# Linear attention feeding a mixture of experts: other queues and cast loads in the opening, one division per head pair, and a layout pass ordered by due times

## The chip, the cores and the metric

The kernel runs on one core of a Trainium2 chip. A core has five engines that run their own instruction streams and wait for each other through semaphores: TensorE (PE: matmuls, with its weight loads shown apart as PEld), VectorE (DVE), ScalarE (ACT), GpSimd (POOL) and SyncE (SP). Three of them, POOL, SP and ACT, can issue DMA transfers; 16 DMA engines carry them. TensorE writes its results to PSUM (here eight banks of 128 x 512 float32), and DVE and ACT read them from there. The metric is the time of one launch on the device in microseconds (us). Smaller is better.

## What is computed

Two stages. Linear attention with the feature map elu + 1 over 8 batches, 8 heads, 576 tokens and 64 values a head; then four experts of two layers each, weighted by a normalised table of probabilities, over the 4608 tokens of all batches:

```python
def _attn_ref(q, k, v):                 # (8, 8, 576, 64) each
    def phi(x):
        return np.where(x > 0, x, np.exp(x) - 1.0) + 1.0
    q_p, k_p = (phi(q), phi(k))
    kv = np.einsum('bhsd,bhse->bhde', k_p, v)
    z = np.sum(k_p, axis=2)
    num = np.einsum('bhsd,bhde->bhse', q_p, kv)
    den = np.einsum('bhsd,bhd->bhs', q_p, z)[..., None] + 1e-06
    return (num / den).astype(np.float32)

def _moe_ref(x, domain_probs, w1, w2):  # x (4608, 512), w1 (4, 512, 1024), w2 (4, 1024, 512)
    p = domain_probs / (domain_probs.sum(-1, keepdims=True) + 1e-09)
    out = np.zeros((N, D), dtype=np.float32)
    for e in range(E):
        h = np.maximum(x @ w1[e], 0.0)
        out += p[:, e:e + 1] * (h @ w2[e])
    return out.astype(np.float32)
```

The attention's output, with heads laid side by side, is the `x` of the second stage.

## The kernel before, in words

**Tiling.** Of the 576 tokens of a batch 512 form a main block (128 partitions of 4 tokens, index `c`) and 64 a rest. The rests of two batches share 128 partitions. Heads go in four pairs (`pr`), so that a pair fills 128 partitions of head values. Work is in float16 with float32 accumulation; the inputs are float32 in memory.

**Attention of one pair** (`attention`, line 382). Three loads bring k, v and q of the pair (`load_pair`, line 258). ACT takes exp of k and of q (412), DVE makes the feature map with two operations each (404, 405), ACT casts v to float16 beside a column of ones (408). PE multiplies k and v (`kv`, 457, and 460 for the 64 rest tokens), so that the product has 2 x 65 columns: values and the sum of k. ACT copies its two diagonal blocks (470, 471). PE transposes q (424), ACT copies the result (437), PE multiplies it by the copied blocks (481), and DVE divides: a reciprocal (495) and a product (497). In the opening the four chunks are divided in two lots, three chunks in the bank `at` and one in the bank `l2b2`. `rest_maps` (313) makes the maps of the 64 rest tokens, with an ACT cast of v (330); `rest_late` (338) finishes the rest of batch 0.

**The opening.** Batch 0 runs while weights still arrive. After each pair's division `turn_x` (579) transposes the new 128 columns of x on PE and ACT copies them (589). `first_l1` (618) then adds that pair's step of layer 1 of expert 0 for four of its eight column blocks (594: four matmuls a pair, one for each of four PSUM banks). After the fourth pair come the other four blocks, then layer 2 (`first_l2`, 655; matmuls 604, weighted sums on DVE 659 to 661). Experts 1 to 3 follow on batch 0, with the attention of batch 1 between them.

**The rest.** Batches 1 to 7 and the rests go through 64 units (`units`, 689). A unit is 256 tokens and one expert, done with seven block products instead of eight in each layer (746 and 822), with sums of weights, of x and of h on DVE. In this part the transposes of q and x are DMA transposes from SP's queue, and the pairs' loads come from SP too.

**Order.** The whole program is first written into a list by `Plan.add`, each operation with its engine, a planned duration, a priority and the keys that it reads and writes. `Plan.order` (55) lays the list out in one pass: it takes the engine that can start first, and on it, of the operations ready by then, the one with the smallest priority number. Priorities are written by hand as times: `T0` and `TU` (138) say that unit n is due at 84.0 + 6.4 n. POOL keeps the order of the list. The engines then run these orders; waits are by semaphores. POOL's DMAs use eight semaphores in turn, so a transfer is issued only when the eighth before it has landed.

**Queues in the opening** (lines 916 to 964). SP loads k, v and q of pair 0. POOL loads, in this order: the rest's k and v of batch 0, pair 1, one slice of w1 of expert 0, pair 2, a slice, pair 3, two slices, the rest's q, the probabilities (one load for the main blocks of all batches, two for the rests), w2 of expert 0, then the weights of expert 1, and so on with batch 1 between. Weights are cast to float16 by their loads. Pair 2 uses as its stage buffers the tiles `xp` and `u2`, which the units use later.

Of the kernel before, what the change touches and what calls it, by code (L numbers as in the profile page):

```python
# [17 lines left out]
BIG = 3.0e38  # L18


class Plan:
# [5 lines left out]

    HOP = 0.28
    NEAR = 0.1
# [24 lines left out]

    def order(self):
        ops = self.ops
# [18 lines left out]
        for _ in ops:  # L75
# [20 lines left out]
            if o["move"]:  # L96
                mover = max(done + o["lead"], mover) + o["move"]
                done = mover + (0.6 if mover < 80 else 2.5)
# [11 lines left out]
def kernel(  # L110
# [27 lines left out]
    T0, TU = 84.0, 6.4  # L138
# [54 lines left out]
    vss.append(u2_b[0].rearrange("p (h c d) -> p h c d", h=2, c=C))  # L193
    xt0 = s4_b[1].rearrange("p a c t -> p a (c t)")
# [63 lines left out]
    def load_pair(b, pr, queue, pri, after=0.0):  # L258
        hs = slice(2 * pr, 2 * pr + 2)
        n = 3 if b < 2 else 2  # L260
        i = rot("stage%d" % n, n) if n == 2 else rot("stage3", 3)
        stage[b, pr] = i
        kk = stage_keys(i)
        for t, o, key in ((k, kqs[i][:, 0], kk[0]), (v, vss[i], kk[2]), (q, kqs[i][:, 1], kk[1])):
            dma(queue, pri, o, t[b, hs, 0:NT].rearrange("h (p c) d -> p h c d", c=C), (key,), 0.7,
                hold=b == 2, after=after)

    def load_rest(b, queue, pri, after=0.0, parts=(0, 1, 2)):
        par = b % 2
        rs = slice(par * R, par * R + R)  # L270
        for i in parts:
            t, o = ((k, kqr[rs, 0]), (v, vr[rs]), (q, kqr[rs, 1]))[i]
            dma(queue, pri, o, t[b, :, NT:S].rearrange("h s d -> s h d"), (("str", par, i),), 0.75,
# [14 lines left out]
    def probs():  # L288
        raw = p5_b[:, 0 : B * C * E].rearrange("p (b c e) -> p b c e", b=B, c=C)
        rrest = sb("prawr", [P, B // 2, E], FP32)  # L290
        src = moe_domain_probs.rearrange("(b s) e -> s b e", s=S)
        dma("POOL", 6, raw, src[0:NT].rearrange("(p c) b e -> p b c e", c=C), ("p5",), 1.5)
        for par in range(2):
            dma("POOL", 6, rrest[par * R : (par + 1) * R],
                src[NT:S].rearrange("s (b t) e -> t s b e", t=2)[par], (("prawr", par),), 0.4)

        def go(r, o, rs, nb):
            nc.vector.tensor_reduce(out=rs, in_=r, axis=mybir.AxisListType.X, op=AO.add)
            nc.vector.tensor_scalar(rs, rs, 1e-9, None, AO.add)
            nc.vector.reciprocal(rs, rs)  # L300
            nc.vector.scalar_tensor_tensor(
                out=o, in0=r, scalar=INV, in1=rs.broadcast_to([P, nb, E]),
                op0=AO.mult, op1=AO.mult,
            )

        rs0, rs1 = sb("prs0", [P, B * C], FP32), sb("prs1", [P, B // 2], FP32)
        pl.add("DVE", 0.6, 24, lambda: go(raw.rearrange("p b c e -> p (b c) e"),
               p_nat.rearrange("p b c e -> p (b c) e"), rs0, B * C), r=("p5",), w=("pnat",))
        pl.add("DVE", 0.4, 60, lambda: go(rrest, p_rest, rs1, B // 2),
# [3 lines left out]
    def rest_maps(b, pe_mode, pri, parts=(0, 1)):  # L313
# [11 lines left out]
        for i in parts:  # L325
# [3 lines left out]
            if i == 0:  # L329
# [52 lines left out]
    def attention(b, pr, pe_mode, pri, step, two=False):  # L382
# [23 lines left out]

        def vcast():
            nc.scalar.copy(vp[:, :, :, 0:D].rearrange("p c h d -> p h c d"), vs)

        order_ = (0, 1)  # L410
        for i in order_:
# [4 lines left out]
            if i == 0:  # L416
                pl.add("ACT", 0.52, pri + step, vcast, r=(sk[2],), w=(("vp", vi),))
# [29 lines left out]
        kvs_, ndk = slot[0], (("at",), ("at",))  # L447
        nds = [slot[0:3], slot[0:2]]
        if two:
            more = [l2b[2][:, i * 2 * DE : (i + 1) * 2 * DE] for i in range(3)]  # L450
            kvs_, ndk = more[0], (("at",), ("l2b2n",))
            nds[1] = more[1:3]
        kvk = ("l2b2k",) if two else ("at",)

        def kv():
            for c in range(C):
                nc.tensor.matmul(  # L457
                    out=kvs_, lhsT=kp[:, c], rhs=vp[:, c], start=(c == 0), stop=False
                )
# [5 lines left out]
                stop=True,  # L465
            )

        def kvcopy():
# [4 lines left out]
        pl.add("PE", 0.3, pri + 4 * step, kv,  # L473
               r=(("kqp", pi, 0), ("vp", vi), ("vpr", par), "kpr"), w=kvk)
# [4 lines left out]
        def nd_mm(u, c0, n):  # L479
            for c in range(c0, c0 + n):  # L480
                nc.tensor.matmul(  # L481
                    out=nds[u][c - c0],
# [6 lines left out]
        def norm(u, c0, n, ri):  # L489
            nd = at[:, 0 : n * 2 * DE]  # L490
            if two and u:
                nd = l2b[2][:, 2 * DE : (2 + 2 * n) * DE]
            nd = nd.rearrange("p (c h e) -> p c h e", c=n, h=2)
# [9 lines left out]
            if n == 2:  # L503
# [7 lines left out]
        for u, (c0, n) in enumerate(((0, 3), (3, 1 if two else 2))):  # L511
            ri = rot("rc", 2)
            pl.add("PE", 0.06 * n, pri + (5 + u) * step, lambda u=u, c0=c0, n=n: nd_mm(u, c0, n),
                   r=(("qT", ti), ("kvz", zi)) + ((("qTr", par, pr),) if n == 2 else ()), w=ndk[u])
            pl.add("DVE", (0.5, 0.74, 0.72)[n - 1], pri + (5.5 + u) * step,
                   lambda u=u, c0=c0, n=n, ri=ri: norm(u, c0, n, ri), r=ndk[u],
                   w=[("x", par, pr, c) for c in range(c0, min(c0 + n, C))]
                   + ([("xr", b, pr)] if n == 2 else []))
# [99 lines left out]
    def first_l1(e, pri, step, wide):  # L618
        ht = []
        banks = [(l1b[i], "l1b%d" % i) for i in range(3)]  # L620
        if wide:
            banks += [(l2b[i], "l2b%d" % i) for i in range(1)]
# [7 lines left out]
        if wide:  # L630
            for dc in range(DC):
                for fj in range(4):
                    bank, key = banks[fj]
# [6 lines left out]
            done = 4  # L640
# [398 lines left out]
```

## Time and profile before

| | us |
|---|---|
| runs before: median of 3 (lowest, highest) | 502.38 (501.99, 503.30) |
| the profiled execution, its own time | 502.13 |
| its span, first to last instruction | 500.4 |

| engine | busy, us |
|---|---|
| DVE | 409.4 |
| ACT | 368.1 |
| POOL | 42.4 |

The profile's page gives busy time by engine, then the span in 40 slices of 12.5 us, where each digit is the busy share of an engine in tenths. These are the slices of the DMA engines and of the granted TensorE clock:

```profile
PEclk9999999999999999999999999999999999999999
DMA  8999957935677597465456685757622432323321
```

The DMA engines are close to full for the first five slices, in which all weights are loaded, and have room later. Below the slices the page has the chain of work that ended last and the costliest groups of instructions. A timeline row reads: start, duration, engine, line, operation, output tile <- input tiles, shape, how many; in brackets how long the engine had been idle and what ended that. Tile names come without buffer numbers: `s` can be `s15` (which also holds the identity) or `s4`, `l2b` any of four banks.

### The profile page before, as it was taken

The numbers are of one execution on the slowest core, as the hardware profiler recorded it, in microseconds if no ns is written. First come the engines' busy times: TensorE is split into PE (matmuls) and PEld (weight loads), VectorE is DVE, ScalarE is ACT, GpSimd is POOL, SyncE is SP. The second block draws the span as 40 slices with busy tenths as digits, with TensorE's granted clock in tenths as the row PEclk, the third lists the DMA queues.
The fourth block names the chain that finished last, engine by engine and source line by source line (L and its number), as shares of the span: only waits on it lengthen the run. The fifth ranks groups of instructions, "written<-read, shape, count | busy, mean of one in ns | idle before, by whom it ended". The sixth has DMA issues, their size and how long they took to land.

```text
span 500.4 us, 14836 instructions
## 1 busy us (share of the span) xinstructions
PE 480.9 (96%) x6008; PEld 423.5 (85%) x6008; DVE 409.4 (82%) x1036; ACT 368.1 (74%) x694; POOL 42.4 (8%) x68
## 2 busy tenths in 40 slices
PE   2799999999999999999999999999999999999995
PEld 1444546999999999999999999999999999999994
DVE  5787997889998999798998898899988676767664
ACT  5738667997987798859886888788866767676641
POOL 8846500000000000000000000000000000000000
PEclk9999999999999999999999999999999999999999
DMA  8999957935677597465456685757622432323321
GB/s 236 233 235 221 264 123 171 262 69 159 145 159 161 128 146 159 114 179 146 127 117 175 120 179 117 132 151 149 160 54 77 53 86 45 86 44 85 39 49 44
DMA packets 124006, 67.51 MB, mean 135 GB/s; under 512 B 94480, under 2 KB 117776, under 8 KB 123936
## 3 DMA queue, kind: packets, MB, share of 16 engines
q1 hardware_dynamic: 115056, 51.53, 46.4%
q0 software_dynamic: 8720, 14.76, 13.9%
q8 instruction: 47, 0.77, 0.6%
q10 hardware_dynamic: 160, 0.26, 0.2%
q14 instruction: 23, 0.19, 0.1%
HBM read 45.16 MB, written 9.44 MB: 109 GB/s over the span
## 4 chain that ended last, share of the span: by engine, by line
PE 90%; DMA 3%; ACT 3%; DVE 2%; issue 1%; POOL 1%; DVEq 0%; POOLq 0%; ACTq 0%
PE l1b L746 39%; PE l2b L822 37%; PE l2b L604 5%; PE l1b L594 5%; DMA w<-in_moe_w_dram 2%; PE at L481 2%; PE at L457 1%; DMA vr<-in_v_dram 1%; ACT xp L706 1%; DVE ot L661 1%; ACT h L760 0%; DVE ot L888 0%; ACT ek L412 0%; PE at L460 0%; ACT p L763 0%
## 5 line engine op out<-in xcount | busy, mean ns | idle before, releaser
L746 PEld LDWEIGHTS <-w 128*128 128x128 f16 x2048 | 132.4, 98 | 4.8
L760 ACT ACTIVATE h<-l1b 128x512 f16<-128x512 f32 x128 | 76.8, 600 | 54.0 <-PE l1b L746 52.5
L822 PE MATMUL l2b<-w,h 128*128 128x256 f16 x768 | 114.9, 273 | 0.1
L822 PE MATMUL l2b<-t,s 128*128 128x256 f16 x768 | 112.6, 273 | 0.0
L746 PEld LDWEIGHTS <-w1x 128*128 128x128 f16 x1536 | 99.9, 98 | 5.1 <-issue 1.5
L822 PEld LDWEIGHTS <-s 128*128 128x128 f16 x1024 | 92.1, 98 | 7.5
L766 DVE CUSTOM_DVE_ANT_0 h<-l1b,p 128x512 f16<-128x512 f32 x64 | 44.1, 690 | 44.9 <-PE l1b L746 40.5
L746 PE MATMUL l1b<-xs,w1x 128*128 128x128 f16 x1024 | 78.1, 219 | 0.5 <-ACT l1b L763 0.3
L746 PE MATMUL l1b<-xT,w 128*128 128x128 f16 x1024 | 78.1, 219 | 0.0
L746 PE MATMUL l1b<-xs,w 128*128 128x128 f16 x1024 | 78.1, 219 | 0.0
L706 ACT ACTIVATE xp<-x,p_nat 128x512 f16<-128x512 f16 x112 | 76.4, 720 | 1.2 <-DMA xT<-xp 0.4
L822 PEld LDWEIGHTS <-h 128*128 128x128 f16 x768 | 67.2, 98 | 5.2 <-ACT h L760 0.3
L808 DVE TENSOR_TENSOR s<-h 128x512 f16<-128x512 f16 x128 | 53.8, 420 | 1.4
L766 DVE CUSTOM_DVE_ANT_0 h<-l1b,u 128x512 f16<-128x512 f32 x64 | 43.8, 684 | 3.5 <-PE l1b L746 2.2
L763 ACT COPY u<-l1b 128x512 f32<-128x512 f32 x64 | 37.4, 584 | 12.5 <-PE l1b L746 12.2
L763 ACT COPY l1b<-l1b 128x512 f32<-128x512 f32 x64 | 36.6, 572 | 13.1 <-PE l1b L746 11.8
L763 ACT COPY p<-l1b 128x512 f32<-128x512 f32 x64 | 37.4, 584 | 8.8 <-PE l1b L746 7.6
L724 DVE TENSOR_TENSOR xs<-xT,xs 128x256 f16<-128x256 f16 x128 | 36.9, 288 | 4.1 <-DVE xs L724 0.5
L412 ACT ACTIVATE ek<-kq 128x512 f16<-128x512 f32 x60 | 37.8, 631 | 2.4 <-DMA kq<-in_k_dram 1.9
L746 PE MATMUL l1b<-xT,w1x 128*128 128x128 f16 x512 | 39.0, 219 | 0.1
L822 PE MATMUL l2b<-w,s 128*128 128x256 f16 x256 | 38.4, 273 | 0.0
L405 DVE TENSOR_TENSOR kqp<-ek,kqp 128x512 f16<-128x512 f16 x64 | 27.2, 425 | 10.6 <-ACT ek L412 7.1
(114 smaller groups left out, 560.7 us busy)
## 6 DMA issues: line engine op xcount, KB each, us to landing
w<-in_moe_w_dram POOLq DMA_DIRECT2D x32, 256.0 KB, 7.5
out_dram<-ot SPq DMA_DIRECT2D x16, 512.0 KB, 3.2
kq<-in_k_dram SPq DMA_DIRECT2D x25, 256.0 KB, 3.1
vs<-in_v_dram SPq DMA_DIRECT2D x25, 256.0 KB, 3.2
kq<-in_q_dram SPq DMA_DIRECT2D x25, 256.0 KB, 3.9
kq<-in_k_dram POOLq DMA_DIRECT2D x5, 256.0 KB, 7.2
vs<-in_v_dram POOLq DMA_DIRECT2D x5, 256.0 KB, 6.6
kq<-in_q_dram POOLq DMA_DIRECT2D x5, 256.0 KB, 6.1
```

Source lines behind the costliest of these rows:

```text
L405: nc.vector.tensor_tensor(out=o, in0=ek[:, i], in1=o, op=AO.min)
L412: pl.add("ACT", 0.55, pri + i * step, lambda i=i: nc.scalar.activation(ek[:, i], kq[:, i], AF.Exp), r=(sk[i],), w=(("ek", ei, i),))
L594: nc.tensor.matmul(out=bank, lhsT=w1_sb[e][:, dc, fj * P : (fj + 1) * P], rhs=xt0[:, dc, :], start=(dc == 0), stop=(dc == DC - 1),)
L604: nc.tensor.matmul(out=bank, lhsT=hts[ht[fj]][:, c * P : (c + 1) * P], rhs=w2_sb[e][:, fj, :], start=(fj == 0), stop=(fj == FC - 1),)
L706: pl.add("ACT", 0.6, pri, lambda c=c, src=src, ps=ps: nc.scalar.activation(xp[:, c, :], src, AF.Copy, scale=ps), r=r, w=(("xp", xi, c),))
L724: lambda o=o, a=a, b_=b_: tt(out=o, in0=a, in1=b_, op=AO.subtract),
L746: nc.tensor.matmul(out=bank[:, fc * P : (fc + 1) * P], lhsT=wt[:, kc, fc * P : (fc + 1) * P], rhs=r[:, kc, :], start=(start and fc == 0 an ...
L760: return lambda: nc.scalar.activation(o, bank, AF.Relu)
L763: return lambda: nc.scalar.copy(o, bank)
L766: return lambda: nc.vector._custom_dve(TENSOR_ADD_SAT, out=o, in0=bank, in1=t, s0=BIG, s1=0.0)
L808: pl.add("DVE", 0.36, U(n + 1) + d - 0.5, lambda i=i, a=a, b_=b_, alu=alu: tt(out=s4[:, i], in0=a, in1=b_, op=alu), r=r, w=(Q(i),))
L822: nc.tensor.matmul(out=l2b[bank][:, half * HD : (half + 1) * HD], lhsT=a[:, c, :], rhs=w[:, c], start=(opens and first and c == 0), stop=( ...
```

## The change

It has six parts.

1. **v cast by its load.** In batch 0 the v of pairs 1 to 3 is loaded from POOL's queue straight into float16 (`v16`), in the first half of its own stage buffer. The v of pair 0 still comes from SP in float32 and is cast by ACT, into `v00`. As v now has no column of ones beside it, `kv` multiplies twice per chunk: 2 x 64 columns of v and 2 columns of a constant tile `ones`.
2. **First rests on other queues.** The rest's k of batch 0 is loaded on ACT's queue, ahead of everything there. Its v is loaded by POOL, cast on the way into `vprs[0]`, behind pair 1's k. All pairs' loads now stand before the four w1 slices; then two batches of probabilities, w2, and only then the rest's q.
3. **One division per pair** in the opening: numerators of all four chunks fill `at`, denominators go to 8 columns of `l2b2`, with one reciprocal and one product for all.
4. **Probabilities in two loads**: batches 0 and 1 in the opening, batches 2 to 7 and the rests at the end of POOL's list, into a buffer that is free by then.
5. **Second layout pass by deadlines**: `order` lays the list out once, computes for each operation not on PE the latest start that still meets the PE starts of that pass, uses it as priority, and lays the list out again.
6. **Priorities and layer shapes**: `T0` becomes 79.0, hand priorities of the opening's layers and of batch 1 move, layer 2 of expert 0 takes four banks instead of three, and the memsets are regrouped.

```diff
+    LAND = 0.6
...
+    def deadlines(self):
+        ops = self.ops
+        late = [o["start"] if o["eng"] == "PE" else BIG for o in ops]
+        for n in range(len(ops) - 1, -1, -1):
+            o = ops[n]
+            for d in o["deps"]:
+                x = ops[d]
+                lat = self.HOP if x["eng"] != o["eng"] or x["move"] else 0.03
+                if x["move"]:
+                    lat += x["lead"] + x["move"] + self.LAND
+                late[d] = min(late[d], late[n] - lat - x["dur"])
+        for n, o in enumerate(ops):
+            if o["eng"] != "PE":
+                o["pri"] = late[n]
+
     def order(self):
+        self.lay_out()
+        self.deadlines()
+        return self.lay_out()
...
-    T0, TU = 84.0, 6.4
+    T0, TU = 79.0, 6.4
...
+    v00 = vss[1].rearrange("p h c d -> p (h c d)").bitcast(FP16)[:, 2 * C * D :].rearrange(
+        "p (h c d) -> p h c d", h=2, c=C
+    )
+    ones = sb("ones", [P, 2, 1], FP16)
...
+    def v16(i):
+        flat = vss[i].rearrange("p h c d -> p (h c d)").bitcast(FP16)
+        return flat[:, 0 : 2 * C * D].rearrange("p (h c d) -> p h c d", h=2, c=C)
...
-        for t, o, key in ((k, kqs[i][:, 0], kk[0]), (v, vss[i], kk[2]), (q, kqs[i][:, 1], kk[1])):
+        vo = vss[i] if b or queue == "SP" else v16(i)
+        for t, o, key in ((k, kqs[i][:, 0], kk[0]), (v, vo, kk[2]), (q, kqs[i][:, 1], kk[1])):
...
+            if first is not None and key == kk[0]:
+                first()
...
+            if b == 0 and i == 1:
+                o, key = vprs[0][rs, :, 0:D], ("vpr", 0)
...
-            if i == 0:
+            if i == 0 and b:
                 pl.add("ACT", 0.55, pri + 0.1, lambda: nc.scalar.copy(
                     vprs[par][rs, :, 0:D], vr[rs]), r=(("str", par, 1),), w=(("vpr", par),))
...
+            if two:
+                nc.scalar.copy(vh, vs)
...
-            if i == 0:
-                pl.add("ACT", 0.52, pri + step, vcast, r=(sk[2],), w=(("vp", vi),))
+            if i == 0 and not (two and pr):
+                pl.add("ACT", 0.52, pri + step, vcast, r=(sk[2],), w=(vk,))
...
+                if two:
+                    nc.tensor.matmul(out=kv3[:, :, 0:D], lhsT=kp[:, c], rhs=vh[:, :, c],
+                                     start=(c == 0), stop=False, skip_group_check=True)
+                    nc.tensor.matmul(out=kv3[:, :, D:DE], lhsT=kp[:, c], rhs=ones,
+                                     start=False, stop=False, skip_group_check=True)
...
+            def nd0():
+                for c in range(C):
+                    nc.tensor.matmul(out=at[:, c * P : (c + 1) * P], lhsT=qT[:, c],
+                                     rhs=kvz[:, :, 0:D], start=True, stop=True)
+                    nc.tensor.matmul(out=den[:, c], lhsT=qT[:, c],
+                                     rhs=kvz[:, :, D:DE], start=True, stop=True)
+
+            def norm0():
+                rc = rc4.rearrange("p (c h) -> p c h", h=2)
+                nc.vector.reciprocal(rc, den)
+                nc.vector.tensor_tensor(
+                    out=xs[:, :, fs].rearrange("p c (h d) -> p c h d", h=2),
+                    in0=at.rearrange("p (c h d) -> p c h d", c=C, h=2),
+                    in1=rc[:, :, :, None].broadcast_to([P, C, 2, D]),
+                    op=AO.mult,
+                )
...
+    load_rest(0, "ACT", 0, parts=(0,))
     load_pair(0, 0, "SP", 0)
-    load_rest(0, "POOL", 0, parts=(0, 1))
-    load_pair(0, 1, "POOL", 0)
-    load_w1(0, (0,))
+    load_pair(0, 1, "POOL", 0, first=lambda: load_rest(0, "POOL", 0, parts=(1,)))
     load_pair(0, 2, "POOL", 0)
-    load_w1(0, (1,))
     rest_maps(0, True, 3, (0,))
     for pr in range(DC):
         if pr == 3:
             load_pair(0, 3, "POOL", 0)
-            load_w1(0, (2, 3))
+            load_w1(0, range(DC))
+            probs(0, 2, p5_b, ("p5",), "pnat0", 24)
+            load_w2(0)
             load_rest(0, "POOL", 0, parts=(2,))
-            probs()
...
-    ht = first_l1(0, 7, 0.7, True)
-    first_l2(0, ht, 28, 0.9, False)
+    ht = first_l1(0, 15, 0.2, 4)
+    first_l2(0, ht, 22, 0.9, True)
...
+    xk = tuple(("xr", b, pr) for b in (6, 7) for pr in range(2))
+    probs(2, B, xr_sb[:, 3].bitcast(FP32), xk, "pnat", U(0) + 10)
+    probs_rest(U(0) + 20)
```

As laid out, PE's order in the opening changes too: the product of k and v of pair 1 now stands before the transposes of pair 0's q, and each pair's numerator matmuls alternate with 2-column ones for the denominators. PE has 32 matmuls more in all, and as many weight loads.

## The prediction

> **What bounds the kernel now.** I read the page's engine totals and slices first, then the engines' busy time by stretch, then the timeline of the opening beside the chain of waits. The page, totals and the slice row of TensorE:
>
> ```profile
> PE 480.9 (96%) x6008; PEld 423.5 (85%) x6008; DVE 409.4 (82%) x1036; ACT 368.1 (74%) x694; POOL 42.4 (8%) x68
> ...
> PE   2799999999999999999999999999999999999995
> ```
>
> TensorE is the bound nearly everywhere, and what it misses lies in the first two slices and the last. By stretch (us, then busy time and instructions of PE, PEld, DVE, ACT, POOL, then granted clock, DMA share, GB/s):
>
> ```profile
> 0.00:24.20 24.20, 11.51 (x80) 6.96 (x81) 15.87 (x52) 15.67 (x32) 20.27 (x36) 1.00 1.02 235
> 24.20:100.00 75.80, 74.66 (x545) 43.18 (x545) 64.58 (x146) 50.88 (x100) 22.10 (x33) 1.00 0.97 213
> 100.00:480.00 380.00, 379.82 (x5200) 359.69 (x5198) 318.85 (x817) 294.92 (x551) 0.00 (x0) 1.00 0.54 119
> 480.00:500.40 20.40, 14.90 (x188) 13.69 (x185) 10.12 (x24) 6.62 (x13) 0.00 (x0) 0.97 0.09 28
> ```
>
> PE idles 12.69 us up to 24.2, then 1.14 up to 100, 0.18 in the next 380 and 5.50 at the end, where the last sums and stores run. The edits don't touch the end: the last dozen instructions of PE, DVE, ACT and SP stand in the same order in both programs. So whatever is gained comes out of 12.69 + 1.14 us, and the steady part can only lose.
>
> Why 24.2: the timeline of the opening (start, us, engine, line, operation, tiles, shape, in brackets the idle time before and its releaser).
>
> ```profile
> 8.04 0.62 ACT L330 CAST vpr<-vr 64x512 f16<-64x512 f32 x1 [0.71 <-DMA vr<-in_v_dram]
> ...
> 8.71 0.27 PE L460 MATMUL l2b<-vpr,kqpr 128*128 128x130 f16 x1 [0.74 <-ACT vpr L330]
> ...
> 11.23 0.58 ACT L437 COPY qT<-l2b 128x512 f16<-128x512 f16 x1
> ...
> 17.02 0.63 PE L594 MATMUL l2b<-s,w 128*128 128x512 f16 x1
> ...
> 19.32 0.38 PE L594 MATMUL l2b<-s,w 128*128 128x512 f16 x1
> ...
> 23.61 0.58 ACT L589 COPY s<-l2b 128x512 f16<-128x512 f16 x1 [1.33 <-PE l2b L584]
> ...
> 24.25 0.81 PE L594 MATMUL l1b<-s,w 128*128 128x512 f16 x3 [0.67 <-DMA w<-in_moe_w_dram]
> ```
>
> Layer 1 of expert 0 goes in four steps, one per head pair of batch 0; from the fourth (24.25) on PE is saturated. The chain of waits puts a weight load before it:
>
> ```profile
> 12.08 6.94 DMA w<-in_moe_w_dram
> 19.02 0.29 issue
> 19.31 4.90 DMA w<-in_moe_w_dram
> 24.21 0.04 issue
> 24.25 0.81 PE l1b L594 x3
> ```
>
> I don't believe it. The slice needed here is the fourth of w1, issued at 12.08 and landed at 19.02; the transfer issued at 19.31 is of the next weights and shares a rotating semaphore. What ended at 24.19 is the ACT copy at 23.61. The opening ends with the attention of pair 3; w1 had been there for 5 us.
>
> **How the sum is made.** PE's work from that fourth step on is the same in both programs (the 32 added matmuls lie before it). So the time moves by (start of the fourth step − 24.25), plus changes of the 1.14 and 0.18 us of later idling.
>
> **Part 1: transfers.** The 16 DMA engines are full from 2.5 us on (share 1.02 over the opening), so data comes in queue order: by issue plus landing, 0.70 us per k, v or q transfer, 1.1 to 1.4 per weight slice. The rest of k moves from POOL (issued 1.29, landed 4.9 later, at 6.16) to ACT's queue at about 0.74. Before shows no ACT load; the near row is SP's load of the same rows at 78.65, which landed in 3.3: that gives 4.0; sharing with k of pair 0 at most 5. I take 4.3. ACT pays one issue of about 0.5 (SP's 0.47 here), ahead of its table load (1.28), both over before the first data: nothing, and 0.5 if data were there at 2.5. The rest of v comes already cast, behind k of pair 1: 7.96 becomes 6.3 (one 0.7 transfer less ahead would give 7.2, both less 6; the ACT cast of 0.62 goes as well). A casting load may move more or less slowly than a plain one; the near row is the w slices, 512 KB read in 1.1 to 1.4 us, the rate of the plain loads, so nothing, with −0.3 to +0.4 per pair.
>
> [...] Then six transfers of 0.70 instead of six and two w slices: q3 lands at 13.8 (before 16.51). w1 now follows all pairs: first slice 15.0 (before 11.05), fourth 18.5 (before 19.02). The first is used at 15.78 before, so 4.7 us of slack shrink to about 1.
>
> **Part 2: attention of batch 0.** Off ACT: three of four v casts (3 x 0.61) and the rest cast (0.62). DVE: a pair's two reciprocals and two products (0.19, 0.56, 0.17, 0.29; 1.19 from start to end at 20.01) become one reciprocal and one 128x512 product: 0.20 + 0.72, from 0.56 for 384 and 0.29 for 128 columns; I take 0.95 with the hop. PE: each pair gets eight 2-column matmuls, each with a weight load of its own. Row: loads of 0.10 us (0.15 cold); no 2-column matmul is shown. Bounds: hidden (0) to 0.15 each; I take 0.11 cold, 0.055 warm, so +0.4 us for kv and +0.4 for the division's matmuls, half that warm.
>
> The path, all in program order. ACT holds exp q1, kvz1's copies, exp k2 before the copy of qT0: 9.5 + 0.52 + 0.43 + 0.52 + 0.58 = 11.55 (before 11.81). Division matmuls 0.61 + 0.4: 12.6. Behind them on PE: turn q1 and kv2 (0.6 + 1.0) to 14.2, turn x0 to 14.8, division of pair 1 to 15.8, turn q2 to 16.3; x0's copy (15.4) and the first w1 slice (15.0) are there. Layer 1 step one 0.9 warm: 17.2. Then kv3 0.65, turn x1 0.25, division of pair 2 0.45 = 18.55; DVE 0.95 + hop = 19.55; turn x2 and two layer-1 matmuls 0.85, division of pair 3 0.45 = 20.85; DVE 0.95 = 21.8; turn x3 0.4, copy 0.6 = **22.8**. Before 24.25: **−1.45 us**.
>
> PE's state is the soft spot. In the rows above the same matmul takes 0.63 at 17.02 and 0.38 at 19.32 with the granted clock at 1.00 throughout. [...]
>
> **Part 3: later weights.** Earlier arrival doesn't help if layer 1 of expert 1 stands waiting. [...] Expert 3's w1 is complete at 63.1 and used at 68.15: 5 us of slack. DVE's w sums stay covered: PE first needs them at 82.
>
> **Part 4: probabilities, memsets, T0.** The opening's four DVE operations (1.09 in sum) shrink to about 0.6 and stand after pair 3's product: off the path. The second load (POOL, idle after 60) is needed from batch 2 on, past 100. Memsets stay before 4.3. All 0. T0 only shifts priorities.
>
> **Part 5: second pass.** It reorders DVE, ACT and SP everywhere. To gain: of the 1.14 us, waits of 0.59 (67.7) and 0.27 (83.9). I take −0.6 in 24 to 100 (bounds −1.1 and +1.5), 0 in the steady part (−0.18 to +6, below). Store and load order on SP is hidden behind loads that are issued tens of us early; a transpose of x behind a late store would cost PE its wait in full.
>
> **Sum.** −1.45 − 0.6 = −2.05: span 500.4 → 498.35. The profiled execution took 502.13, 1.7 more than its span, and the median is 502.38: **500.1 us**, −0.45%. About 0.3% (1.5 us) is what a measurement of this kernel can tell from no change.
>
> **Rivals.**
> A, the forecast: 0.40, 499.0 to 501.2.
> B, more: PE is fast early, pairs run through without ACT's order holding them, both idle rests vanish: fourth step at 21 to 21.5 and −1.1: 497.0 to 498.5, limit by part 3. For it: ACT had 8.5 us idle in the opening. Against: its order puts loads' exps before qT copies. 0.20.
> C, hidden anyway: q0 slips to 9, PE stays cold and runs 32 more matmuls; fourth step at 23.8 to 24.5, rest as before: 501.2 to 503.5. For it: DMA full, part 2's PE additions. 0.23.
> D, slower: the second pass ranks by due times from planned durations that are too short (DVE sums 0.36 planned, 0.42 in the row, four per unit; relu sums 0.62 and 0.69, two per unit: 0.38 us of DVE per unit). Work is then placed that much too late and the steady part gets a wait per unit. 64 units at 0.1 us: +6.4, less 2: 506.5. It decides from 0.06 per unit, 3.5 us between 100 and 480. For it: DVE 84% busy there. Against: 61 us of DVE air, and PE's order alternates the two layers more evenly in the new program. 0.17.
>
> Chances: faster = B + nearly all of A = 0.57; same = C and A's tail = 0.26; slower = D = 0.17. The range, 497.0 to 503.6, leaves out D's far side and little of B; A alone is 499.0 to 501.2.
>
> **What would show it.** Right: k rest landed by 5, q3 by 14.5; step one of layer 1 waiting for neither w1 nor DMA; fourth step at 22.3 to 23.6; idle of PE in 24:100 under 1.1 and in 100:480 under 0.5. Wrong: first step waiting for its w1 slice (then everything behind it on PE waits, kv3 and the pairs too), layer 1 of expert 1 waiting for DMA, or idle of PE beyond 3 us in 100:480.

## The result and the profile after

| us | median | lowest to highest | runs |
|---|---|---|---|
| before | 502.25 | 501.99 to 503.30 | 4 |
| after | 499.63 | 499.00 to 500.29 | 4 |

The ratio is 0.9944, with a 95% interval of 0.9925 to 0.9963: 2.6 us faster, and the forecast of 500.1 lies 0.5 us above the measured median. The profiled execution took 499.62 with a span of 497.8 (before 502.13 and 500.4). The same kernel, run once more beside the experiments, gave 499.26.

The page after, the rows of TensorE in the totals and the slices:

```profile
PE 479.3 (96%) x6040; PEld 424.8 (85%) x6040; DVE 411.1 (83%) x1033; ACT 366.9 (74%) x690; POOL 42.5 (9%) x68
...
PE   1899999999999999999999999999999999999995
```

PE has its 32 matmuls more and is still bound nearly everywhere; the slices are too coarse to show where 2.5 us went. The busy time by stretch, cut at the start of the fourth step of layer 1 (columns as before: PE, PEld, DVE, ACT, POOL, granted clock, DMA share, GB/s):

```profile
0.00:22.75 22.75, 10.70 (x112) 7.88 (x113) 14.26 (x44) 13.31 (x27) 16.76 (x30) 1.00 1.07 215
22.75:100.00 77.25, 76.55 (x578) 45.28 (x578) 66.78 (x155) 53.75 (x105) 25.70 (x38) 1.00 0.99 214
100.00:480.00 380.00, 379.70 (x5202) 360.35 (x5201) 321.58 (x817) 295.03 (x550) 0.00 (x0) 1.00 0.54 119
480.00:500.40 20.40, 12.38 (x153) 11.32 (x150) 8.44 (x18) 4.78 (x9) 0.00 (x0) 0.94 0.09 27
```

PE idles 0.70 us between the cut and 100 (before 1.14) and 0.30 in the next 380 (before 0.18), so the feared wait in every unit did not come. The timeline of the opening, rows of PE, ACT and DVE:

```profile
9.00 0.27 PE L519 MATMUL l2b<-vpr,kqpr 128*128 128x130 f16 x1 [1.20 <-DMA vpr<-in_v_dram]
...
12.38 0.29 PE L544 MATMUL at<-kvz,qT 128*128 128x128 f16 x1 [1.36 <-ACT qT L493]
...
15.97 0.88 PE L677 MATMUL l1b<-s,w 128*128 128x512 f16 x3 [0.25 <-ACT s L672]
...
19.11 0.59 PE L677 MATMUL l1b<-s,w 128*128 128x512 f16 x2 [0.89 <-ACT s L672]
...
20.71 0.21 DVE L551 RECIPROCAL rc<-l2b 128x8 f32<-128x8 f32 x1 [1.29 <-PE l2b L546]
20.95 0.69 DVE L552 TENSOR_TENSOR x<-at,rc 128x512 f16<-128x512 f32 x1
...
22.14 0.59 ACT L672 COPY s<-l2b 128x512 f16<-128x512 f16 x1 [1.59 <-PE l2b L667]
...
22.77 0.81 PE L677 MATMUL l1b<-s,w 128*128 128x512 f16 x3 [0.67 <-ACT s L672]
```

The first step of layer 1 stands at 15.97 (before 15.78), the fourth at 22.77 (before 24.25). No step waits for weights. The last four rows belong to the chain that sets the opening's end: one division of 0.94 us, four transposes (at 21.70, not shown), one copy, the step.

Every program has the same 5928 matmuls from the fourth step on. So two differences split the change of the span: the start of that step, and the stretch from there to the end. Spans are taken to hundredths from the trace.

| kernel (profiled execution) | q of pair 1 landed | first step | fourth step | fourth step to end | span |
|---|---|---|---|---|---|
| before | 9.95 | 15.78 | 24.25 | 476.11 | 500.36 |
| after | 9.82 | 15.97 | 22.77 | 475.07 | 497.84 |
| after, taken again | 9.74 | 15.75 | 22.50 | 474.98 | 497.48 |

So 1.48 us of the 2.52 come from the opening and 1.04 from behind it. Of the 1.04, 1.05 appear between the first matmul of the first unit and that of the third: 82.55 to 94.35 before, 81.29 to 92.04 after. From there to the end the two traces run 0.21 us apart in sum.

The profile shows only 0.3 of the 1.04 as idle time of PE. The rest counts as busy: the same 5928 matmuls are busy for 469.4 us before and for 468.6 after. The ends of matmuls are modelled, so a short wait can hide in a busy row; it is seen from one start to the next, as below.

What the 1.48 us of the opening are made of is shown only in part. The parts that were put back one at a time also got a new order from the layout pass, and the landings and the clock moved between executions.

### The profile page after: what moved, and what is told of

Its sections match the earlier page's. It is cut to its first block, busy times and chain, and to the rows that moved or that the text cites. A ratio compares the mean times of both kernels' runs of the same rounds, so it can differ in the third digit from the quotient of the medians.

```text
span 497.8 us, 14890 instructions
## 1 busy us (share of the span) xinstructions
PE 479.3 (96%) x6040; PEld 424.8 (85%) x6040; DVE 411.1 (83%) x1033; ACT 366.9 (74%) x690; POOL 42.5 (9%) x68
## 3 DMA queue, kind: packets, MB, share of 16 engines
q0 software_dynamic: 9760, 14.17, 14.0%
## 4 chain that ended last, share of the span: by engine, by line
PE 92%; ACT 2%; DVE 2%; DMA 1%; issue 1%; POOL 0%; DVEq 0%; POOLq 0%; ACTq 0%
PE l1b L831 40%; PE l2b L907 38%; PE l1b L677 5%; PE l2b L687 4%; PE at L567 2%; DMA vpr<-in_v_dram 1%; PE at L516 1%; ACT xp L791 1%; DVE ot L973 0%; ACT s L672 0%; DVE kqp L453 0%; DVE kqp L452 0%; PE at L519 0%; PE l2b L511 0%; DVE x L580 0%
## 5 line engine op out<-in xcount | busy, mean ns | idle before, releaser
L831 PEld LDWEIGHTS <-w 128*128 128x128 f16 x2048 | 134.2, 98 | 5.4
L907 PE MATMUL l2b<-t,s 128*128 128x256 f16 x768 | 114.7, 273 | 0.0
L907 PEld LDWEIGHTS <-s 128*128 128x128 f16 x1024 | 90.1, 98 | 6.2
L791 ACT ACTIVATE xp<-x,p_nat 128x512 f16<-128x512 f16 x112 | 77.6, 721 | 0.5
L848 ACT COPY u<-l1b 128x512 f32<-128x512 f32 x64 | 37.4, 585 | 11.2 <-PE l1b L831 10.9
L893 DVE TENSOR_TENSOR s<-s,h 128x512 f16<-128x512 f16 x64 | 27.1, 424 | 6.3 <-ACT h L845 0.5
```

Of the source, the lines that this page charges most:

```text
L791: pl.add("ACT", 0.6, pri, lambda c=c, src=src, ps=ps: nc.scalar.activation(xp[:, c, :], src, AF.Copy, scale=ps), r=r, w=(("xp", xi, c),))
L831: nc.tensor.matmul(out=bank[:, fc * P : (fc + 1) * P], lhsT=wt[:, kc, fc * P : (fc + 1) * P], rhs=r[:, kc, :], start=(start and fc == 0 an ...
L848: return lambda: nc.scalar.copy(o, bank)
L893: pl.add("DVE", 0.36, U(n + 1) + d - 0.5, lambda i=i, a=a, b_=b_, alu=alu: tt(out=s4[:, i], in0=a, in1=b_, op=alu), r=r, w=(Q(i),))
L907: nc.tensor.matmul(out=l2b[bank][:, half * HD : (half + 1) * HD], lhsT=a[:, c, :], rhs=w[:, c], start=(opens and first and c == 0), stop=( ...
```

## Experiments

All times, each with its ratio to runs of the kernel before that were made beside it. Those had medians between 502.43 and 503.06, so ratios compare better than medians:

| run | median, us | ratio | 95% interval |
|---|---|---|---|
| after_again | 499.26 | 0.9935 | 0.9915 to 0.9955 |
| after_one_pass | 501.02 | 0.9969 | 0.9952 to 0.9985 |
| before_two_pass | 500.83 | 0.9968 | 0.9957 to 0.9979 |
| after_dve_due | 500.62 | 0.9955 | 0.9943 to 0.9967 |
| after_act_casts | 499.10 | 0.9946 | 0.9928 to 0.9964 |
| after_old_rests | 500.09 | 0.9955 | 0.9940 to 0.9971 |
| after_two_lots | 500.55 | 0.9959 | 0.9944 to 0.9974 |
| after_two_lots_2 | 500.23 | 0.9955 | 0.9938 to 0.9973 |
| after_old_slices | 501.21 | 0.9970 | 0.9956 to 0.9984 |
| after_warm | 501.70 | 0.9990 | 0.9970 to 1.0009 |
| after_kept_busy | 501.78 | 0.9982 | 0.9968 to 0.9996 |
| after_kept_busy_2 | 499.31 | 0.9930 | 0.9917 to 0.9942 |

### The second pass, taken out and added alone

The changed kernel with one pass, and the kernel before with nothing but the second pass:

```diff
-        self.lay_out()
-        self.deadlines()
         return self.lay_out()
```

> The changed kernel with its layout laid out once, by the hand priorities; everything else kept. ACT's order in the opening is the same. Theory (the second pass did nothing in the opening and gave the 1.06 us between the start of unit 0 and the start of unit 2): fourth step of layer 1 at 22.8 as in the changed kernel, unit 0 at 81.3 to 81.6, then 0.8 to 1.1 us lost up to unit 2; 500.5 us. Rival (T0 and the moved priorities smoothed the start of the units, the pass is idle): unit 2 at 92.0, 499.6 us.

> The kernel before with the second pass by due times alone. Theory: fourth step of layer 1 at 24.2, unit 0 at 82.3 to 82.6, 0.8 to 1.1 us gained from unit 0 to unit 2, steady part as before; 501.2 us. Rival (the pass needs the new T0, or gives nothing): 502.2 us; rival D of the prediction (due times too late, a wait per unit): over 504 us.

Alone the pass brings a ratio of 0.9968; all the rest of the change, without it, 0.9969. Their product is 0.9937, and the whole change measured 0.9944 and 0.9935: the two halves add, each about 1.6 us. The traces say where.

In the opening of the changed kernel the pass does nothing that shows. With one pass the fourth step stood at 21.86, not at 22.8 as expected, but q of pair 1 had also landed early, at 9.06. Behind that landing it came after 12.80 us, in the two profiles of the changed kernel after 12.95 and 12.76. In the kernel before the pass moved the fourth step from 24.25 to 24.02.

From the fourth step to the end one pass takes 476.67 us, which is 1.60 more than the changed kernel and 0.56 more than the kernel before. The pass added to the kernel before takes 475.17, which is 0.94 less. So in these profiles the other edits to the order lose about half a microsecond behind the fourth step, and the pass makes good that and one more. The stretch 80 to 90 in the kernel before, in the changed kernel and with one pass (PE busy, clock, DMA share, GB/s):

```profile
80.00:90.00 10.00, 9.52 (x113) 1.00 0.95 260
```

```profile
80.00:90.00 10.00, 10.00 (x133) 1.00 1.03 234
```

```profile
80.00:90.00 10.00, 8.22 (x113) 1.00 1.07 254
```

And what PE waited for there with one pass (who waits <- for whom, us in total, times, longest):

```profile
PE l1b L829 <- DVE h L849: 0.7, 1, 0.7
PE l1b L829 <- DVE xs L807: 0.4, 1, 0.4
PE l1b L829 <- ACT l1b L846: 0.4, 1, 0.4
PE l1b L829 <- ACT u L846: 0.2, 1, 0.2
```

These are the first units' sums of x and h on DVE and copies on ACT. The two engines also have batch 2's attention and the last sums of batch 0 in hand, and the hand priorities put some of those first. With due times PE shows no idle time in this stretch.

Part of the waits is hidden in busy rows. In the kernel before, four matmuls of 256 columns are followed after 0.44 us where nothing is waited for, and at 88.88 after 0.73:

```profile
88.44 0.60 PE L822 MATMUL l2b<-t,s 128*128 128x256 f16 x4
88.88 0.60 PE L822 MATMUL l2b<-w,h 128*128 128x256 f16 x4
89.61 0.61 PE L746 MATMUL l1b<-xT,w1x 128*128 128x128 f16 x8
```

The chain of waits before says for what. ACT takes an exp and a cast of batch 2's attention ahead of the copy that PE's next row needs:

```profile
87.80 0.63 ACT ek L412
88.43 0.52 ACT vp L408
...
88.97 0.59 ACT p L763
89.56 0.04 issue
89.61 0.61 PE l1b L746 x8
```

An estimate from the starts, between the first matmul of the first unit and that of the third: the time beyond what the same matmuls take where nothing waits (0.45 us for eight of 128 columns, 0.44 for four of 256) is 1.5 us before, 0.5 in the changed kernel, 1.0 with the pass added to the kernel before, and 2.6 with one pass.

### Due times on DVE alone

```diff
-            if o["eng"] != "PE":
+            if o["eng"] == "DVE":
                 o["pri"] = late[n]
```

> The changed kernel with two passes, but the due times become priorities on DVE alone; ACT and SP keep the hand priorities. What is read is the stretch from the fourth step of layer 1 to the end of the span: 475.07 and 474.98 in the two profiles of the changed kernel, 476.67 with one pass. Theory (it is the DVE sums of weights and x at the start of the units that one pass lays out too late): 475.3 or less, 499.0 to 500.0 in time. Rival (the gain needs ACT's copies or SP's transfers in due order too): 476.2 or more, 500.5 to 501.3.

From the fourth step to the end it took 475.70: 0.97 of the 1.60 us come back, 0.63 do not, so neither theory holds alone. At 86.40 PE still waits 0.42 us for h, whose sums follow ACT's copies. In this execution the first step ran at the slow rate (three matmuls in 1.44 us from 15.84), and the fourth stood at 23.34.

### v cast by ACT again

v of all pairs is loaded as float32 and cast by ACT beside the column of ones; the rest of v stays a casting load.

```diff
-        vo = vss[i] if b or queue == "SP" else v16(i)
+        vo = vss[i]
...
-            vh = v00 if pr == 0 else v16(si)
+            vh = vp[:, :, :, 0:D].rearrange("p c h d -> p h c d")
...
-            if i == 0 and not (two and pr):
+            if i == 0:
```

> The changed kernel with v of pairs 1 to 3 loaded in float32 and cast by ACT; same load order. Theory (the opening hangs on ACT's order behind q1): one cast of 0.52 to 0.6 us now stands before the copy of qT0 and one or two more before later copies; fourth step 0.6 to 1.2 us later, 23.4 to 24.0; 500.5 us. Rival (casts fall into ACT's idle time, the loads' order made the gain): fourth step at 22.8 to 23.0, 499.6 us.

The three casts are back on ACT:

```profile
8.80 0.63 ACT L461 CAST vp<-vs 128x512 f16<-128x512 f32 x1
...
11.57 0.63 ACT L461 CAST vp<-u 128x512 f16<-128x512 f32 x1
...
13.61 0.64 ACT L461 CAST vp<-vs 128x512 f16<-128x512 f32 x1
```

The time is the changed kernel's: 499.10 against 499.63 and 499.26, with intervals that overlap almost wholly. The fourth step stood at 21.96 in its one profile, not at 23.4 to 24.0; q of pair 1 had landed early (9.15), and behind that landing it came after 12.81 us, as in the changed kernel (12.95 and 12.76). The theory fell: moving the casts off ACT earned nothing that can be told. The casts are not the only difference, though. The layout also gave ACT another order: here the copy of x of pair 0 (14.17) runs ahead of two copies and an exp of later pairs, in the changed kernel (15.33) behind them.

The landings say what the transfers paid. In the changed kernel the cast v of pairs 2 and 3 landed 0.43 and 0.46 us after the k ahead of it; here, plain, 0.75 each. So the casting load was 0.3 us a pair shorter, though its packets are busy for longer in sum (256 of about 60 ns against 64 of 176 to 191, over 16 engines 0.96 us against 0.70 to 0.76). Packet times overlap (the DMA share of the opening is 1.07), so their sum is not what the queue waits for.

### The rests on their old queues

```diff
-    load_rest(0, "ACT", 0, parts=(0,))
     load_pair(0, 0, "SP", 0)
-    load_pair(0, 1, "POOL", 0, first=lambda: load_rest(0, "POOL", 0, parts=(1,)))
+    load_rest(0, "POOL", 0, parts=(0, 1))
+    load_pair(0, 1, "POOL", 0)
```

The rest's v is also plain again, with its ACT cast.

> The changed kernel with the rest's k and v of batch 0 loaded by POOL ahead of pair 1, plain, with ACT's cast of v, as before. Theory (ACT's order waits for q1, which lands at 9.8 to 10 either way; the first product of k and v is off the path): fourth step 21.8 to 23.4 as in the changed kernel, within 0.3 us of it in time, 499.6 us. Rival (the rests' queues made the opening's gain): first step 0.5 to 1.5 us later, 500.8 us.

500.09, and intervals that overlap. By the ratios 0.5 to 1.0 us may be lost, which isn't told apart from none. The fourth step stood at 22.75, the same, though q of pair 1 had landed 0.3 us earlier (9.46). In the changed kernel the rest's v landed at 8.96 (plain in the kernel before: 7.96) and held PE for 1.20 us, the row at 9.00 above. ACT waited for that product and still ended its two copies at 9.74, before q of pair 1 landed at 9.82, so nothing was lost there.

### Two lots in the division

The changed kernel, with the division in lots of three chunks and one as before. It was run twice.

```diff
+            lots = (
+                (0, 3, at[:, 0:384], at[:, 384:390], "at", 0.27, 0.74),
+                (3, 1, l2b[2][:, 384:512], l2b[2][:, 256:258], "l2b2n", 0.09, 0.5),
+            )
```

> The changed kernel with the division in two lots again, chunks 0 to 2 and chunk 3, each with reciprocal and product. Theory (DVE's division of pairs 2 and 3 is on the path once each, 1.19 instead of 0.9 us): fourth step 0.4 to 0.6 us later than in the changed kernel, 500.1 us. Rival (the one division carries the opening's gain): 1.2 us or more later, 500.9 us.

> The kernel with the division in two lots once more, unaltered. In its first profile the granted clock was released only at 20.69, so the fourth step (24.14) mixes the division with the clock. Theory (two lots cost 0.4 to 0.6 us, the rest was the clock's phase): with a release before 18.9 the fourth step is at 22.7 to 23.3; 500.0 us. Rival (the division itself costs 1.2 us or more): fourth step at 23.7 or later at any release, 500.6 us.

The last pair, in the timeline of DVE, ACT and PE:

```profile
21.99 0.20 DVE L555 RECIPROCAL rc<-at 128x6 f32<-128x6 f32 x1 [0.70 <-PE at L550]
...
22.22 0.56 DVE L556 TENSOR_TENSOR x<-at,rc 128x384 f16<-128x384 f32 x1
22.69 0.16 DVE L555 RECIPROCAL rc<-l2b 128x2 f32<-128x2 f32 x1
...
22.89 0.29 DVE L556 TENSOR_TENSOR x<-l2b,rc 128x128 f16<-128x128 f32 x1
...
23.50 0.58 ACT L679 COPY s<-l2b 128x512 f16<-128x512 f16 x1 [1.41 <-PE l2b L674]
...
24.14 0.59 PE L684 MATMUL l1b<-s,w 128*128 128x512 f16 x2 [0.67 <-ACT s L679]
```

Two lots take 1.19 us here, one division 0.94. The fourth step stands at 24.14 and 24.37, 1.4 to 1.9 later than in the two profiles of the changed kernel. That is more than three divisions at 0.25. In both profiles PE also stayed at the slow rate for longer: the clock was released at 20.69 and 21.11 (16.15 and 15.82 with one division), and in the first of them three matmuls of the first step took 1.44 us from 16.07 (0.88 from 15.97 with one division). In the second the first step also waited for its weights (landed at 16.20). These runs cannot separate the causes. Behind the fourth step 0.4 us come back (474.67 and 474.65 to the end, where PE no longer waits at 66.4). By the ratios the time is 0.5 to 1.2 us longer, with intervals that overlap.

### The w1 slices between the pairs again

```diff
+    load_w1(0, (0,))
     load_pair(0, 2, "POOL", 0)
+    load_w1(0, (1,))
...
-            load_w1(0, range(DC))
+            load_w1(0, (2, 3))
```

> The changed kernel with the w1 slices of expert 0 between the pairs' loads as before: slice, pair 2, slice, pair 3, two slices. Pair 2 lands 1.1 and pair 3 2.2 us later (q3 at about 16 instead of 13.7). Theory (with ACT lightened, pairs 2 and 3 are held by their loads; putting all pairs first made most of the opening's gain): third and fourth step 0.8 to 1.5 us later, about 23.4, 500.8 us. Rival (compute-bound from pair 1 on, loads are early anyway): fourth step within the scatter of the changed kernel, 499.6 us.

501.21 and 0.9970: by the ratios 1.3 to 1.8 us lost, the largest loss of any part of the opening (its nine runs lie between 499.48 and 501.95; its interval overlaps the changed kernel's first one narrowly and the second one not at all). The first step came early (14.05, with q of pair 1 at 8.82) and the fourth late (23.34). q of pair 3 landed at 15.52 (13.68 in the changed kernel), but no row of PE, ACT or DVE between 11.2 and 23.3 waits for a transfer. What differs is the order that was laid out for the later loads: exp of q3 starts at 17.33, 1.8 us after its landing (14.68 in the changed kernel), and PE's third step now stands ahead of the division's matmuls of pair 3. The changed kernel, then this one:

```profile
20.19 0.22 PE L544 MATMUL at<-s,qT 128*128 128x128 f16 x1
...
20.60 0.81 PE L677 MATMUL l1b<-s,w 128*128 128x512 f16 x3
```

```profile
19.83 0.81 PE L677 MATMUL l1b<-s,w 128*128 128x512 f16 x3 [0.22 <-ACT s L672]
...
20.69 0.22 PE L544 MATMUL at<-s,qT 128*128 128x128 f16 x1
```

So PE had little to do behind the third step. Three stretches of its profile (columns as in the table by stretch above):

```profile
21.02:24.43 3.41, 1.60 (x13) 0.72 (x11) 3.05 (x6) 1.26 (x3) 1.42 (x3) 1.00 1.17 229
24.43:27.85 3.42, 3.42 (x9) 1.19 (x9) 2.57 (x5) 2.50 (x5) 2.61 (x4) 0.50 1.13 208
27.85:31.26 3.41, 3.41 (x17) 1.53 (x16) 1.93 (x4) 1.79 (x3) 2.01 (x4) 1.00 1.23 205
```

In the first PE is busy for 1.60 of 3.41 us. In the second the granted clock is 0.50, and nine matmuls fill it; the third, as long and at 1.00, holds 17. From the fourth step (23.34) to the start of layer 2 of expert 1 it takes 20.56 us, in the changed kernel 18.88. Of these 1.7 us most come back later: to the end it takes 475.61, only 0.54 more than in the changed kernel. So the profiled execution loses 0.6 at the fourth step and 0.5 behind it.

### PE kept busy early

Three kernels ask whether the slow rate of PE at the start (in the changed kernel 0.27 us for a 128x128 matmul at 14.99, 0.22 at 16.90) holds the opening back. All add 128x128 matmuls into a PSUM bank that nothing reads before layer 1; they add no value to the output. The first adds 48 ahead of the first data, the second some 140 spread over PE's waits, both on the tile `kqpr`.

```diff
+    def busy(n):
+        for _ in range(n):
+            nc.tensor.matmul(out=l1b[2][:, 0:P], lhsT=kqpr[:, 0, 0:2].rearrange("p h d -> p (h d)"),
+                             rhs=kqpr[:, 1, 0:2].rearrange("p h d -> p (h d)"), start=True, stop=True)
```

> The changed kernel with 48 added matmuls of 128 columns on a zeroed tile at the start of PE's stream, between 1.5 and 6.7 us, when PE has nothing to do; they add no value to the output. Theory (PE is slow up to about 15.5 us because it was idle, and this is on the path from 12.4 on): matmuls after 7 us take half the start-to-start time (128 columns in 55 instead of 107 ns), first step of layer 1 at 14.9, when its weights land, fourth step 0.7 to 1.1 us earlier, about 21.9; 498.7 us. Rival (ACT and the landings set every step, PE's speed is hidden): fourth step 22.6 to 22.8, 499.6 us.

> The changed kernel with matmuls of 128 columns on a zeroed tile at PE's start (72) and in its waits of the opening (20 and 8 around the rest's product of pair 0, 22 behind the turn of q0, 12 and 8 further on, all before the first step of layer 1); they add no value to the output. [...] Rival (the added matmuls stand in the way of real ones, or ACT sets the pace): fourth step at 22.5 or later, 499.5 us or more.

Neither settles it; both came out slower than the changed kernel (501.70 and 501.78). `kqpr` also receives the map of the rest's k, so DVE had to wait for the added matmuls before writing it, and the first product of k and v slipped from 7.11 to 7.83 and 10.04. after_warm also lost 1.8 us behind the fourth step (476.84 to the end), which isn't explained. It does show the clock, by stretch:

```profile
1.12:4.53 3.41, 3.04 (x29) 3.04 (x30) 2.47 (x13) 1.28 (x1) 3.11 (x5) 1.00 0.84 183
4.53:7.94 3.41, 1.36 (x25) 1.19 (x23) 1.92 (x5) 2.66 (x5) 2.45 (x5) 1.00 1.38 270
7.94:11.35 3.41, 1.88 (x22) 1.53 (x20) 2.74 (x8) 2.53 (x8) 3.11 (x5) 0.50 1.13 315
11.35:14.77 3.42, 3.07 (x37) 2.89 (x37) 2.34 (x6) 3.10 (x8) 3.42 (x7) 0.50 1.15 218
```

PE is busy for 3.04 us of the first stretch and 1.36 of the second; in the two behind 7.94 the granted clock is 0.50. A 128x128 matmul took 0.23 us at 7.83, 0.27 at 7.92 and 0.22 again from 18.18. The third kernel repeats the second on a zeroed tile of its own, with 60 matmuls ahead of the data and 70 in the waits:

```diff
+    zz = sb("zz", [P, P], FP16)
...
+            nc.tensor.matmul(out=l1b[2][:, 0:P], lhsT=zz, rhs=zz, start=True, stop=True)
```

> The changed kernel with about 130 added 128x128 matmuls in the opening on a zeroed tile of its own, which no other instruction writes: 60 before the first data, the rest in PE's waits. They add no value to the output. Theory (slow matmuls hold the opening back): the clock is released by 8.3 and stays open; first step of layer 1 at 15.0 or before, fourth at 21.3 to 22.0 (22.77 and 22.50 in the two profiles of the changed kernel), 498.3 to 499.0. Rival (loads and ACT's order set the pace, and PE's speed is worth nothing before 16): first step at 15.7 or later, fourth at 22.4 or later, 499.3 to 500.3.

```profile
0.99 5.04 PE L288 MATMUL l1b<-zz 128*128 128x128 f16 x60 [0.99 <-DVE zz L1010]
...
16.05 0.81 PE L686 MATMUL l1b<-s,w 128*128 128x512 f16 x3 [0.53 <-ACT s L681]
...
19.13 0.59 PE L686 MATMUL l1b<-s,w 128*128 128x512 f16 x2 [0.89 <-ACT s L681]
...
22.79 0.81 PE L686 MATMUL l1b<-s,w 128*128 128x512 f16 x3 [0.67 <-ACT s L681]
```

Now PE is fast from the first product on (128x128 matmuls of 0.22 us from 6.61, 0.27 without), and the steps stand where they stood: 16.05, 19.13, 22.79 against 15.97, 19.11, 22.77. 499.31 us is the changed kernel's time. The theory of a PE that holds the opening back before 16 falls. What the first step follows is q of pair 1: 6.15 and 6.01 us after its landing in the two profiles of the changed kernel, 6.00 here (10.05 to 16.05), 6.03 with one pass (9.06 to 15.09). Between them lie ACT's exps and copies; in the changed kernel ACT is busy in 6.44 of the 7.10 us from 9.3 to 16.4. The transposes of x of pair 0 end at 14.72, and ACT copies them from 15.33 on, when two copies and an exp of later pairs are done.

### The changed kernel again

Nothing is edited.

> The changed kernel once more, unaltered, for the scatter of the opening between executions. [...] Rival (the opening is the same every time): release at 16.1, fourth step at 22.7 to 22.8.

499.26, clock released at 15.82, first step at 15.75, fourth at 22.50: 0.2 to 0.4 us from the first profile at each mark. A single profile can be further off. In the profiles with the same loads q of pair 1 landed anywhere from 9.06 to 10.05, and the marks of the opening move with it. No experiment was told apart from the changed kernel as faster.

## Why the prediction was right, point by point

- **Bound and where to look.** Right in place: the gain lies at the start of the fourth step and between there and 100; the steady part lost 0.12 us and the end nothing. The rule that behind the fourth step only idle time can change was too narrow: idle time gave 0.3 of the 1.04 us, and the rest, by the estimate from the starts, were waits inside busy rows.
- **Fourth step, 22.8.** Measured 22.77 and 22.50. That it met so closely is in part luck. The copy of qT0 ended at 12.33 instead of 11.55, the division's matmuls at about 13.1 instead of 12.6, the first step started at 15.97 instead of 16.3; from the first to the fourth it took 6.80, forecast 6.5. The errors cancel, and the scatter of the landings alone is larger.
- **Part 1, landings.** q of pair 3: 13.8 forecast, 13.68 measured; the plain transfers behind q of pair 1 took about 0.75 rather than 0.70, and the cast ones less. q of pair 1: no run shows the 9.5 that the path starts from as what the new loads bring; it landed at 9.82, 0.13 earlier than before (9.06 to 10.05 over the profiles with the same loads). w1's first slice 15.0, measured 14.84; the fourth 18.5, measured 19.98, unneeded until 22.77. k rest 4.3, measured 4.85. v rest 6.3 was wrong by 2.7 us, and without cost. Putting the slices back lost more than any other part of the opening, but through a new order; what the earlier landing of pairs 2 and 3 is worth by itself is not shown.
- **The rest's k on ACT's queue.** It came 1.31 us earlier (4.85 against 6.16), and q of pair 1 gained 0.13. q0 landed at 8.00 and 8.34, 0.3 to 0.65 later than before, but it scatters by more than that with the same loads (7.29 to 8.71). Putting the rests back cost nothing that can be told.
- **Casting load, nothing with −0.3 to +0.4.** By the landings −0.3 a pair, at the edge of the bounds. ACT without its three casts brought no gain that can be told.
- **Division, 0.95.** Measured 0.94. The 2-column matmuls start 0.07 us apart from their neighbours at the slow rate, so four cost 0.28 where 0.4 was taken.
- **PE's state.** The path counts the first step as warm, 0.9 us; no row of before shows it (1.66 there, 15.78 to 17.44, with the release at 17.79). Measured 0.93 (15.97 to 16.90), with the release at 16.15, and at 15.82 in the second profile. Before 16 the rate was worth nothing (after_kept_busy_2). Behind it, it can be: in two profiles where the first step ran at the slow rate (after_dve_due, after_warm: 1.44 us for three matmuls) the fourth came 7.50 and 8.08 us after the first instead of 6.80. Both programs differ in other things too.
- **Part 3.** Right: the last w1 slice of expert 1 landed at 30.62 and its layer 1 began at 32.78. The limit that rival B takes from this part is shown by no run; nothing waited for that slice.
- **Part 4.** Right: the four operations on the probabilities stand at 21.56 to 22.4, behind pair 3's product. That `T0` costs nothing was wrong: with one pass, the new priorities and the rest of the new order cost 0.56 us behind the fourth step.
- **Part 5, −0.6.** The mis-sized term, and luck in its reason. Of the two waits that it counted on, the first is still there:

```profile
66.43 0.40 PE L480 MATMUL l2b<-s,kqp 128*128 128x128 f16 x4 [0.59 <-DVE kqp L453]
```

  The gain is at the units' start: −1.04 in the stretch behind the fourth step, −1.60 against the same program with one pass. Of about 1.5 us of waits between the first and the third unit before, the profile showed 0.48 as idle time of PE in 80 to 90, and the forecast counted 0.27 of that.
- **Rival D** fell: idle in 100 to 480 is 0.30. **C** fell: the fourth step came at 22.77, q0 landed at 8.0 to 8.3, and a fast PE did not move the marks, so its 32 matmuls are hidden. **B** had the right reason, ACT's order, on the wrong side: that order still holds the first step.

The sum was −2.05 in span, measured −2.52; −1.45 became −1.48, and −0.6 became −1.04.

## What to carry to other kernels

Split a change at a mark behind which both programs do the same work, and compare the start of that mark and the stretch behind it: here one subtraction showed that two fifths of the gain lie behind the opening. What an ordering pass can bring is more than the idle time that the profile shows on the bound engine. Read the waits from one start to the next, above all at a change of phase, where two jobs share the helper engines, and run the pass by itself. Where the program is laid out anew at every edit, putting a part back also changes the order, so look at the order before calling the part the cause. A resource that looks slow (PE, with 0.27 us for a 128x128 matmul against 0.22 later) is tested by making it fast at no other cost, on data that nothing else touches.

## What the runs showed of the hardware

In the openings one and the same matmul had two durations. In the kernel before, a 128x512 matmul took 0.63 us at 17.02 and 0.38 at 19.32, and the trace has the first release of the clock at 17.79. In the changed kernel a 128x128 matmul took 0.27 us at 14.99 and 0.22 at 16.90, with the release at 16.15; in its second profile the release came at 15.82. With two lots it came at 20.69 and 21.11, and in the first of these profiles a 128x128 matmul took 0.27 us at 19.13 and 0.22 at 21.64. What sets the moment is not shown.

The row of the granted clock is 1.00 over the whole opening of both kernels (0 to 24.20 before, 0 to 22.75 after), through the slow matmuls and the fast ones alike. Later changes it does show: 0.50 from 7.94 to 18.18 in after_warm and from 24.43 to 27.85 in after_old_slices. So in these openings the durations tell the rate, not the row.

The cost of a casting load was told by its landing, not by the sum of its packets' times: a v of 256 KB in memory, cast to float16, landed 0.43 and 0.46 us after the transfer ahead of it (after), and plain 0.75 (after_act_casts), though the packets of the cast one were busy for longer in sum (0.96 us over 16 engines against 0.70 to 0.76).
